# The residual gate's product in the last two blocks: seven half products in place of eight, between the first output products

## The chip, the core and the metric

The kernel runs on one core of one Trainium2 chip. The metric is the device time of one execution in microseconds (us). The engines are TensorE (PE, matmuls; its weight loads are shown apart as PEld), VectorE (DVE), ScalarE (ACT), GpSimd (POOL) and SyncE (SP, which issues transfers here).

## The reference

Attention without a softmax, an RMS norm per head, and a gated feed-forward with a gated residual:

```python
kv  = einsum('bhsd,bhse->bhde', k, v)          # 8 batches, 8 heads, 576 tokens, 64 wide
o   = einsum('bhsd,bhde->bhse', q, kv)
x   = (o / sqrt(mean(o*o, -1) + 1e-6) * g_norm) # -> 4608 tokens x 512
ffn = (gelu(x @ w_gate) * (x @ w_val)) @ w_out  # 512 -> 1536 -> 512
out = x + sigmoid(x @ w_res) * ffn              # w_res: 512 x 512
```

The change touches only `x @ w_res` and what surrounds it.

## The kernel before, in words

The 4608 tokens are worked in nine blocks of 512. Blocks 0 to 7 are the first 512 tokens of each batch; block 8 gathers the last 64 tokens of all batches. `x` lies in `xT`, transposed, in fp16: four token quarters j of 128 tokens, and four parts cc of 128 of the 512 features. Each block has two stages.

*Hidden stage.* `gv_group` (line 708) forms four of the twelve 128-wide slices of the hidden layer, for gate (g) and value (v). It uses a Strassen-Winograd scheme: a product of 2 x 2 quadrants is made with seven half products in place of eight, from sums of weight quadrants (made once) and differences of token quadrants (`token_sums`, line 688, kept in `ts`, new for each block). A half product is here four matmuls of 256 columns. The order of the work is a string of words in `ORDERS` (line 703): a digit and a factor is a half product ("6g"), E is a copy by ACT that seeds one PSUM bank with product 1 (line 747), d a copy by ACT to SBUF (line 751), F and c additions by DVE (line 758), "g11" a gelu by ACT (line 768), "h11" the product of gate and value (line 774, on DVE, and for "h22" on POOL). The last group's order ends "... 4g g12 h12 4v g21 h22 h21". Lists keyed by a word (`amid`) hang other work behind it.

*Output stage.* `m_res` (line 412) forms `x @ w_res` for one token quarter with four matmuls of 512 columns (line 415, tile `rps`) and ACT takes the tanh of half of it into `th` (line 424). Later `m_sigmoid` (line 427) turns that into a sigmoid (line 429). `out_by_products` (line 497) then forms the output product with w_out, also in seven half products, but these have twelve matmuls of 256 columns each (`prod`, line 484, matmuls on line 488): A, D, A, E, A, F, A by the names of the tiles. They read the hidden layer itself (`a_of`) or four sums of its quadrants, `hid_s`, made by DVE on line 463, each 128 x 1536: s2 in `s_begin` (line 470, hung at word "h12" of the last group), s0 and s1 in `s_rest` (line 475), s3 in `s_last` (line 481). ACT copies A to E (line 515, `wE`) and D to SBUF (line 518, `wd`); DVE adds A and `wd` to F (`wF`).

`out_last` (line 577) does the same for block 8, with smaller pieces at the end: the copies are lines 612 and 614, POOL makes `u` from `th`, `wd` and x, DVE gates (line 589), POOL or DVE add x (line 593), and SP and ACT each issue four stores (line 598), in the order in which the pieces are done.

Nothing is planned by a scheduler: each engine runs its instructions in the order of the program text, and waits on the others through semaphores. PSUM has eight banks; `banks_of` (line 1263) names those of blocks 7 and 8 by hand. In these two blocks, `LAST` on line 644, no attention work is left, and the four `rps` tiles have banks of their own. The order on PE around the change is: last group's 4g, 4v; sixteen `rps` matmuls; products A, D, A, E, A, F, A. On ACT: gelu of "g21", four tanh, copy `wE`, copy `wd`, four sigmoids (in block 8: four tanh, two sigmoids, two half copies of `w`, `wd`, two sigmoids). On DVE: h11, h12, s2, h21, s0, s1, s3.

Of the kernel before, what the change touches and what calls it, by code (L numbers as in the profile page):

```python
# [8 lines left out]
FP32 = mybir.dt.float32  # L9
FP16 = mybir.dt.float16  # L10
# [8 lines left out]
def kernel(  # L19
# [15 lines left out]
    nc = tc.nc  # L35
# [439 lines left out]
    def s_rest(blk):  # L475
# [2 lines left out]
        sub(nc.vector, s_[0], a_of(blk, 2, 1), a_of(blk, 2, 2), ALU.add)  # L478
        sub(nc.vector, s_[1], s_[0], a_of(blk, 1, 1))

    def s_last(blk):
        sub(nc.vector, hid_sums[3], a_of(blk, 1, 2), hid_sums[1])

    def prod(ps, a, b, start, es=(0, 1)):

        for e in es:
            for f in range(NFH):
# [6 lines left out]
                    skip_group_check=True,  # L494
                )

    def out_by_products(blk, later, banks, amid):
        w = {}
        s_ = hid_sums

        def aside(ahead_of):
            for f in amid.get(ahead_of, ()):
                f()

        def res(jj):
            for j in (2 * jj, 2 * jj + 1):
                m_res(blk, j, banks[j])

        def first_two():
            for n in ("D", "E", "F", "A"):  # L510
                w[n] = pmoe.tile([P, 2, CH], FP32, name="w" + n, bank=banks[n])
            w["d"] = attnp.tile([P, 2, CH], FP32, tag="sq", bufs=3, name="wd")
            s_last(blk)
# [24 lines left out]
        def others():  # L538


            prod(w["A"], s_[1], wo_t[:, 1], False)
            aside("F")
            sub(nc.vector, w["F"], w["A"], w["d"], ALU.add)
            aside("00")
            prod(w["E"], a_of(blk, 1, 2), b_of(2, 1), False)
            pf((0, 0), w["E"])
            aside("22")
            prod(w["A"], s_[2], wo_t[:, 2], False)
            c22 = res_all[part((1, 1))]
# [12 lines left out]
            if later:  # L562
                return
            for i in (1, 0):
                fin((i, i))
                fin((i, 1 - i))
                store(i)

        if later:
            x = [lambda j=j: a_x(blk, j) for j in range(NJ)]  # L570
            at_word(blk + 1, 0, "1v", *x[0:2], lambda: fin((0, 0)), lambda: fin((0, 1)), lambda: store(0))
            at_word(blk + 1, 0, "Fv", x[2])
            at_word(blk + 1, 0, "cv", x[3])
            at_word(blk + 1, 0, "h22", lambda: fin((1, 0)), lambda: fin((1, 1)), lambda: store(1))
        return [lambda: res(0), lambda: res(1), first_two, others]

    def out_last(blk, banks):

        s_ = hid_sums

        def bank(n, i):
            return pmoe.tile([P, n, CH], FP32, name="w", bank=i)

        def part(j, n, ch):
            return slice(None), slice(j, j + n), slice(ch * CH, (ch + 1) * CH)

        def gated(j, n, ch, src):
            of = part(j, n, ch)
            nc.vector.tensor_tensor(out=res_all[of], in0=th_all[of], in1=src, op=ALU.mult)

        def plus(j, n, ch, eng):
            of = part(j, n, ch)
            eng.tensor_tensor(out=res_all[of], in0=res_all[of], in1=t_t[blk][of], op=ALU.add)

        def store(j, n, c0, c1):
            for e, queue in enumerate((nc.sync, nc.scalar)):
                dst = out.rearrange("(j e s) c -> e s j c", e=2, s=S)[e, M0:S, j : j + n, c0:c1]
                queue.dma_start(out=dst, in_=res_all[e * R : (e + 1) * R, j : j + n, c0:c1])

        def run():  # L600
            wa = [bank(1, banks["A"][e]) for e in range(2)]
            wd, we, wf = [bank(2, banks[n]) for n in "DEF"]
            d = attnp.tile([P, 2, CH], FP32, tag="sq", bufs=3, name="wd")
            u = attnp.tile([P, 2, CH], FP32, tag="sq", bufs=3, name="u")
            one = (slice(0, 1), slice(1, 2))
            s_last(blk)
            for e in range(2):
                prod(wa[e], a_of(blk, 1, 1), b_of(1, 1), True, (e,))
            for j in (2, 3):
                m_sigmoid(j)  # L610
            for e in range(2):
                nc.scalar.copy(out=we[:, one[e], :], in_=wa[e])
            prod(wd, s_[0], wo_t[:, 0], True)
            nc.scalar.copy(out=d, in_=wd)
# [12 lines left out]
            gated(0, 2, 1, wf)  # L627
            plus(0, 2, 1, nc.gpsimd)
            store(0, 2, CH, C)
            for e in range(2):  # L630
                prod(wa[e], s_[2], wo_t[:, 2], False, (e,))
                gated(2 + e, 1, 1, wa[e])
            of = part(2, 2, 1)
            sub(nc.vector, res_all[of], res_all[of], u, ALU.add)
            store(2, 2, CH, C)
            for e in range(2):
                prod(wa[e], a_of(blk, 2, 2), wo_t[:, 3], False, (e,))
                gated(2 + e, 1, 0, wa[e])
                plus(2 + e, 1, 0, nc.vector)
            store(2, 2, 0, CH)  # L640

        return [lambda: [m_res(blk, j, banks[j]) for j in range(NJ)], run]

    LAST = (B - 1, B)
    GF = 4
# [526 lines left out]
    def at_word(blk, i, word, *fs):  # L1172
        amid_gv.setdefault((blk, i), {}).setdefault(word, []).extend(fs)
# [80 lines left out]
    for blk in GROUPS:  # L1254
        t = token_sums(blk, nc.vector)
        if blk == 2:
            at(blk - 1, NF + 3, *t)
            continue
        for key, f in zip(("00", "00", "22", "01") if whole(blk) else ("00", "22", "01", "11"), t):
            aside_out(blk - 1, key, f)  # L1260
    out_at = {}

    def banks_of(blk):
# [35 lines left out]
    for blk in range(B + 1):  # L1299
# [21 lines left out]
        else:  # L1321
            slots = [lambda f=f: m_gval(blk, f) for f in range(NF)]
            groups = GROUPS.get(blk, ())
            if groups:
                n = NF - GF * len(groups)
                slots[n:] = [None] * (NF - n)
                ends = []
                at_word(blk, len(groups) - 1, "h12", lambda: s_begin(blk))

                def group(i, blk=blk, ends=ends):  # L1330
                    if i == 0:
# [20 lines left out]
                plan.setdefault(NFH + 2, []).insert(0, lambda: s_begin(blk))  # L1352

            def products(blk=blk, outs=outs):
                s_rest(blk)
                if blk not in GROUPS:
                    out_at[blk] = banks_behind()
                if blk < B:
                    outs.extend(out_by_products(blk, blk == 1, out_at[blk], amid_out.get(blk, {})))
                else:  # L1360
                    outs.extend(out_last(blk, out_at[blk]))
# [54 lines left out]
```

## Time and profile before

| what | us |
|---|---|
| median of three runs (324.31 to 324.40) | 324.36 |
| the profiled execution, its own time | 324.4 |
| its span | 322.6 |
| PE busy | 314.9 |
| DVE busy | 263.5 |
| ACT busy | 201.5 |
| POOL busy | 144.9 |
| `rps` stage of block 7, starts | 273.40 to 276.86 |
| `rps` stage of block 8, starts | 304.37 to 307.82 |

How to read the rows that follow: a timeline row has start, duration, engine, line, operation, output <- inputs, shape and count. Where the engine had been idle, brackets give how long and which engine's instruction ended the wait. A matmul row's duration includes a modelled drain: rows in a stream overlap, and the pace is read from start to start. Rows of stretches (windows) have, after the engines' busy times, the granted PE clock, the share of the 16 DMA engines that was busy, and GB/s.

### The profile page before, as it was taken

The page shows a single profiled execution, that of the slowest core. Times are in us where ns is not written, and L with a number is a line of the kernel's source. Part 1 is how long each engine was busy: PE and PEld are TensorE (multiplying, and loading weights), DVE is VectorE, ACT ScalarE, POOL GpSimd, SP SyncE. Part 2 cuts the span into 40 slices and gives each one's busy share as a digit, 9 for nine tenths or more (in the row PEclk, how much of TensorE's full clock was granted, in tenths as well). Part 3 has the DMA queues.
Part 4 walks back from the last instruction along what each step waited for, and adds up shares of the span by engine and source line. Part 5 has one row for each costly group of instructions (what it writes and reads, how often), then busy time and mean ns, then how long its engine had stood idle before and what let it go on. Part 6 is the DMA issues. An engine that isn't in the chain of part 4 may idle for free.

```text
span 322.6 us, 7458 instructions
## 1 busy us (share of the span) xinstructions
PE 314.9 (98%) x2936; PEld 236.6 (73%) x2936; DVE 263.5 (82%) x482; ACT 201.5 (62%) x367; POOL 144.9 (45%) x212
## 2 busy tenths in 40 slices
PE   8999999999999999999999999999999999999993
PEld 3555754444857878887888688868887888788782
DVE  5788869799799887998799879998896777677754
ACT  3773676365737784878486848684766467636760
POOL 2792342573702779247833784117511342042232
PEclk9999999999999999999999999999999999999998
DMA  8999999798995599399938993810321030002004
GB/s 255 325 204 204 194 205 180 168 193 121 162 130 108 170 139 101 122 165 123 108 132 162 112 121 131 136 33 2 130 47 36 2 130 4 0 34 101 0 2 130
DMA packets 76693, 38.89 MB, mean 121 GB/s; under 512 B 42098, under 2 KB 74354, under 8 KB 76658
## 3 DMA queue, kind: packets, MB, share of 16 engines
q0 software_dynamic: 38752, 17.17, 42.5%
q1 hardware_dynamic: 37328, 20.71, 24.9%
q8 instruction: 23, 0.38, 0.5%
q10 hardware_dynamic: 578, 0.52, 0.5%
q14 instruction: 12, 0.10, 0.1%
HBM read 38.80 MB, written 9.44 MB: 150 GB/s over the span
## 4 chain that ended last, share of the span: by engine, by line
PE 96%; DVE 3%; issue 0%; DVEq 0%
PE Av L737 12%; PE Ag L737 12%; PE wA L488 11%; PE rps L415 10%; PE gps L395 6%; PE vps L395 6%; PE Fv L737 6%; PE Fg L737 6%; PE fps L432 3%; PE Ev L737 3%; PE wE L488 3%; PE wD L488 3%; PE Eg L737 3%; PE wF L488 3%; PE w L488 2%; PE idle L902 2%
## 5 line engine op out<-in xcount | busy, mean ns | idle before, releaser
L774 POOL TENSOR_TENSOR hid<-ge,c 128x512 f16<-128x512 f16 x21 | 24.4, 1163 | 68.5 <-ACT ge L768 68.5
L531 POOL TENSOR_TENSOR osb<-osb,t 128x512 f32<-128x512 f32 x28 | 31.6, 1159 | 36.1 <-DVE osb L527 25.2
L488 PEld LDWEIGHTS <-hid_s 128*128 128x128 f16 x384 | 37.5, 98 | 4.4
L737 PEld LDWEIGHTS <-wsv 128*128 128x128 f16 x336 | 32.8, 98 | 4.4
L737 PEld LDWEIGHTS <-wsg 128*128 128x128 f16 x336 | 32.8, 98 | 3.8
L415 PE MATMUL rps<-wr,xT 128*128 128x512 f16 x144 | 33.4, 380 | 0.0
L488 PEld LDWEIGHTS <-hid 128*128 128x128 f16 x288 | 28.2, 98 | 5.0
L747 ACT COPY Eg<-Ag 128x512 f32<-128x512 f32 x21 | 12.2, 582 | 25.9 <-PE Ag L737 25.9
L758 DVE TENSOR_TENSOR Fg<-Ag,d 128x512 f32<-128x512 f32 x21 | 14.6, 697 | 16.5 <-ACT d L751 11.2
L383 ACT ACTIVATE ge<-gps 128x512 f16<-128x512 f32 x24 | 14.1, 597 | 21.3 <-PE gps L395 21.1
L737 PEld LDWEIGHTS <-wg 128*128 128x128 f16 x252 | 24.4, 98 | 3.7 <-issue 0.4
L737 PEld LDWEIGHTS <-wv 128*128 128x128 f16 x252 | 24.6, 98 | 3.3 <-issue 0.2
L424 ACT ACTIVATE th<-rps 128x512 f32<-128x512 f32 x36 | 21.1, 595 | 8.1 <-PE rps L415 8.0
L737 PE MATMUL Ag<-ts,wsg 128*128 128x256 f16 x168 | 25.2, 273 | 0.0
L737 PE MATMUL Av<-ts,wsv 128*128 128x256 f16 x168 | 25.2, 272 | 0.0
L254 DVE TENSOR_REDUCE ss<-sq 128x8 f32<-128x512 f32 x32 | 20.1, 678 | 5.8 <-ACT sq L249 5.8
L415 PEld LDWEIGHTS <-xT 128*128 128x128 f16 x144 | 13.5, 98 | 14.2
L395 PE MATMUL gps<-xT,wg 128*128 128x512 f16 x88 | 22.6, 379 | 0.0
L395 PE MATMUL vps<-xT,wv 128*128 128x512 f16 x88 | 22.6, 379 | 0.0
L488 PE MATMUL wA<-wo_ts,hid_s 128*128 128x256 f16 x168 | 20.6, 273 | 0.0
L384 DVE TENSOR_TENSOR hid<-ge,vps 128x512 f16<-128x512 f16 x24 | 16.3, 684 | 4.8 <-PE vps L395 4.0
L429 ACT ACTIVATE th<-th 128x512 f32<-128x512 f32 x36 | 20.1, 642 | 0.0
(188 smaller groups left out, 764.7 us busy)
## 6 DMA issues: line engine op xcount, KB each, us to landing
out_dram<-osb SPq DMA_DIRECT2D x14, 512.0 KB, 2.6
qraw<-in_q_dram POOLq DMA_DIRECT2D x7, 512.0 KB, 7.1
k<-in_k_dram POOLq DMA_DIRECT2D x7, 512.0 KB, 10.2
v<-in_v_dram POOLq DMA_DIRECT2D x7, 512.0 KB, 11.4
wg<-in_moe_w_gate_dram POOLq DMA_DIRECT2D x2, 512.0 KB, 8.3
wv<-in_moe_w_val_dram POOLq DMA_DIRECT2D x2, 512.0 KB, 8.8
wo<-in_moe_w_out_dram POOLq DMA_DIRECT2D x2, 512.0 KB, 14.2
out_dram<-osb SPq DMA_DIRECT2D x4, 256.0 KB, 4.9
```

Of the source, the lines that this page charges most:

```text
L254: nc.vector.tensor_reduce(out=out_, in_=sqs.pop((b, i)), op=ALU.add, axis=mybir.AxisListType.X)
L383: nc.scalar.activation(out=ge, in_=gps, func=AF.Gelu)
L384: nc.vector.tensor_tensor(out=hids[blk][:, f, :], in0=ge, in1=vps, op=ALU.mult)
L395: nc.tensor.matmul(ps[:, j0 * P : j1 * P], lhsT=w[:, cc, :], rhs=xT_t[blk][:, j0:j1, cc, :], start=(cc == 0 and j0 == 0), stop=(cc == NP - ...
L415: nc.tensor.matmul(rps, lhsT=xT_t[blk][:, j, cc, :], rhs=wr16[:, cc, :], start=(cc == 0), stop=(cc == NP - 1),)
L424: nc.scalar.activation(out=th, in_=rps, func=AF.Tanh, scale=0.5)
L429: nc.scalar.activation(out=th, in_=th, func=AF.Copy, scale=0.5, bias=0.5)
L488: nc.tensor.matmul(ps[:, e - es[0], :], lhsT=a[:, f, e * P : (e + 1) * P], rhs=b[:, f, :], start=(start and e == es[0] and f == 0), stop=( ...
L531: nc.gpsimd.tensor_tensor(out=res_all[of], in0=res_all[of], in1=t_t[blk][of], op=ALU.add)
L737: nc.tensor.matmul(out_[:, r, :], lhsT=lhsT, rhs=rhs, start=(first and r == 0 and c == 0), stop=(c == 1), skip_group_check=True,)
L758: nc.vector.tensor_tensor(out=dst, in0=ps["A", u], in1=sb["d", u], op=ALU.add)
L774: eng.tensor_tensor(out=dst, in0=ge[q], in1=source(q, "v"), op=ALU.mult)
```

## The change

In blocks 7 and 8, `x @ w_res` is made with the seven-product scheme too (`res_halves`), and its products are laid among the first w_out products.

- Four sums of w_res quadrants (`wr_sums`) are made once, by DVE in block 6, ahead of that block's w_out product D; they lie in the buffer of `qT`, which the attention no longer uses.
- The token differences `ts` of the block are used again.
- The order is the string in `res_halves`; a number is a half product of four matmuls of 256 columns. "sE" and "sd" are ACT copies, "+F" and "+c" DVE additions, "tE" and so on the tanh of a quadrant. Behind "6" comes s0, behind "+F" s1 and the first w_out product A with its copy `wE`, behind "+c" s2 and s3, behind "tF" the first half of the w_out product D. After the string come the second half of D, the copy `wd` and the sigmoids. In block 8, where the two sigmoids of quarters 2 and 3 stood ahead of the copies of `w`, these copies now come first, then the four tanh, the two sigmoids, and then `wd`.
- `s_begin`, `s_rest` and `s_last` are no longer called for these blocks; `s_sum(blk, i)` makes s0 to s3 one at a time. The order on DVE becomes h11, h12, h21, s0, rF, s1, rc, s2, s3.
- On PE: products 1, 5, 6; w_out product A; 2, 7, 3; half of D; 4; the other half of D. From there on as before.
- POOL's and SP's instructions and their order stay the same.

```diff
+    def wr_sums(eng):
+        def one(n, x, y, op=ALU.subtract):
+            if n == 0:
+                wr_s.append(attnp.tile([P, 4, 2, CH], FP16, tag="qT", bufs=1, name="wrs"))
+            x_, y_ = (wr_s[0][:, t] if isinstance(t, int) else wr_quadrant(*t) for t in (x, y))
+            sub(eng, wr_s[0][:, n], x_, y_, op)
...
+    def res_halves(blk, banks, amid):
...
+        def product(p):
+            n = {1: "A", 2: "E", 3: "F", 4: "A", 5: "F", 6: "A", 7: "A"}[p]
...
+            for e in range(2):
+                for cc in range(2):
+                    nc.tensor.matmul(
+                        out_[:, e, :],
+                        lhsT=x_[:, e, cc, :],
+                        rhs=w_[:, cc, :],
...
+        for word in "1 sE 5 sd 6 +F 2 tE 7 +c 3 tF 4 tc tA".split():
+            n = word[-1]
+            if word.isdigit():
+                product(int(word))
+            elif word == "sE":
+                nc.scalar.copy(out=bank("E"), in_=ps["A"])
+            elif word == "sd":
+                sb["d"] = attnp.tile([P, 2, CH], FP32, tag="sq", bufs=3, name="rd")
+                nc.scalar.copy(out=sb["d"], in_=ps["F"])
+            elif word[0] == "+":
...
+                nc.vector.tensor_tensor(out=bank("F") if n == "F" else sb["c"], in0=ps["A"], in1=sb["d"], op=ALU.add)
+            else:
+                tanh(n)
+            for f in amid.get(word, ()):
+                f()
...
+        def with_res():
+            res_halves(blk, dict(zip("AFE", (banks[j] for j in range(3)))), {
+                "6": [lambda: s_sum(blk, 0), tiles_of_w],
+                "+F": [lambda: s_sum(blk, 1), lambda: prod(w["A"], a_of(blk, 1, 1), b_of(1, 1), True),
+                       lambda: nc.scalar.copy(out=w["E"], in_=w["A"])],
+                "+c": [lambda: s_sum(blk, 2), lambda: s_sum(blk, 3)],
+                "tF": [lambda: half_d(0)],
+            })
+            half_d(1)
+            nc.scalar.copy(out=w["d"], in_=w["D"])
+            for j in range(NJ):
+                m_sigmoid(j)
...
+        if res_in_halves(blk):
+            return [with_res, lambda: None, lambda: None, others]
         return [lambda: res(0), lambda: res(1), first_two, others]
...
+            res_halves(blk, dict(zip("AFE", (banks[j] for j in range(3)))), {
+                "6": [lambda: s_sum(blk, 0)],
+                "+F": [lambda: s_sum(blk, 1), ahead],
+                "+c": [lambda: s_sum(blk, 2), lambda: s_sum(blk, 3)],
+                "tF": [lambda: half_d(0)],
+            })
...
-            s_last(blk)
-            for e in range(2):
-                prod(wa[e], a_of(blk, 1, 1), b_of(1, 1), True, (e,))
+            half_d(1)
             for j in (2, 3):
                 m_sigmoid(j)
-            for e in range(2):
-                nc.scalar.copy(out=we[:, one[e], :], in_=wa[e])
-            prod(wd, s_[0], wo_t[:, 0], True)
             nc.scalar.copy(out=d, in_=wd)
...
-        return [lambda: [m_res(blk, j, banks[j]) for j in range(NJ)], run]
+        return [lambda: None, run]
...
+    aside_out(LAST[0] - 1, "D", *wr_sums(nc.vector))
...
-                at_word(blk, len(groups) - 1, "h12", lambda: s_begin(blk))
+                if not res_in_halves(blk):
+                    at_word(blk, len(groups) - 1, "h12", lambda: s_begin(blk))
...
-                s_rest(blk)
+                if not res_in_halves(blk):
+                    s_rest(blk)
```

More of the change, by code (lines that the diff above doesn't have):

```diff
@@ L479, in s_rest, with s_sum @@
         sub(nc.vector, s_[1], s_[0], a_of(blk, 1, 1))
+    def s_sum(blk, i):
+        s_ = hid_sums
+        if i == 0:
+            sub(nc.vector, s_[0], a_of(blk, 2, 1), a_of(blk, 2, 2), ALU.add)
+        elif i == 1:
+            sub(nc.vector, s_[1], s_[0], a_of(blk, 1, 1))
+        elif i == 2:
+            sub(nc.vector, s_[2], a_of(blk, 1, 1), a_of(blk, 2, 1))
+        else:
+            sub(nc.vector, s_[3], a_of(blk, 1, 2), s_[1])
     def s_last(blk):
@@ L495, in prod, with wr_quadrant @@
                 )
+    wr_s = []
+    def wr_quadrant(i, k):
+        return wr16[:, 2 * k : 2 * k + 2, i * CH : (i + 1) * CH]
+    def wr_sums(eng):
[4 more added lines that the diff above has]
+            sub(eng, wr_s[0][:, n], x_, y_, op)
+        return [
+            lambda: one(0, (1, 0), (1, 1), ALU.add),
+            lambda: one(1, 0, (0, 0)),
+            lambda: one(2, (0, 0), (1, 0)),
+            lambda: one(3, (0, 1), 1),
+        ]
@@ new lines, in res_halves, with bank, tanh @@
+    def res_halves(blk, banks, amid):
+        ps, sb = {}, {}
+        def bank(n):
+            ps[n] = pmoe.tile([P, 2, CH], FP32, name="r" + n, bank=banks[n])
+            return ps[n]
+        def product(p):
+            n = {1: "A", 2: "E", 3: "F", 4: "A", 5: "F", 6: "A", 7: "A"}[p]
+            first = p in (1, 5)
+            out_ = bank(n) if first else ps[n]
+            s_of = {3: 3, 5: 0, 6: 1, 7: 2}
+            t_of = {4: 3, 5: 0, 6: 1, 7: 2}
+            quad = {1: (0, 0), 2: (0, 1), 4: (1, 1)}
+            xq = {1: (0, 0), 2: (1, 0), 3: (1, 1)}
+            w_ = wr_s[0][:, s_of[p]] if p in s_of else wr_quadrant(*quad[p])
+            x_ = x_sums[blk][:, t_of[p]] if p in t_of else x_quadrant(blk, *xq[p])
+            for e in range(2):
[4 more added lines that the diff above has]
+                        rhs=w_[:, cc, :],
+                        start=(first and e == 0 and cc == 0),
+                        stop=(cc == 1),
+                        skip_group_check=True,
+                    )
+        def tanh(n):
+            i, j = {"E": (0, 0), "F": (0, 1), "A": (1, 0), "c": (1, 1)}[n]
+            src = sb[n] if n == "c" else ps[n]
+            th = th_all[:, 2 * j : 2 * j + 2, i * CH : (i + 1) * CH]
+            nc.scalar.activation(out=th, in_=src, func=AF.Tanh, scale=0.5)
+        for word in "1 sE 5 sd 6 +F 2 tE 7 +c 3 tF 4 tc tA".split():
[8 more added lines that the diff above has]
+            elif word[0] == "+":
+                if n == "c":
+                    sb["c"] = attnp.tile([P, 2, CH], FP32, tag="o32", bufs=3, name="rc")
+                nc.vector.tensor_tensor(out=bank("F") if n == "F" else sb["c"], in0=ps["A"], in1=sb["d"], op=ALU.add)
+            else:
+                tanh(n)
+            for f in amid.get(word, ()):
+                f()
@@ L497, in out_by_products, with res_in_halves @@
+    def res_in_halves(blk):
+        return blk in LAST
     def out_by_products(blk, later, banks, amid):
@@ L507, in res, with tiles_of_w @@
                 m_res(blk, j, banks[j])
-        def first_two():
+        def tiles_of_w():
             for n in ("D", "E", "F", "A"):
@@ L512, in first_two, with half_d @@
             w["d"] = attnp.tile([P, 2, CH], FP32, tag="sq", bufs=3, name="wd")
+        def half_d(e):
+            prod(w["D"][:, e : e + 1], s_[0], wo_t[:, 0], e == 0, (e,))
+        def with_res():
[10 more added lines that the diff above has]
+                m_sigmoid(j)
+        def first_two():
+            tiles_of_w()
             s_last(blk)
@@ L600, in run, with ahead, half_d @@
         def run():
-            wa = [bank(1, banks["A"][e]) for e in range(2)]
-            wd, we, wf = [bank(2, banks[n]) for n in "DEF"]
+            wa, w = [], []
+            one = (slice(0, 1), slice(1, 2))
+            def ahead():
+                wa.extend(bank(1, banks["A"][e]) for e in range(2))
+                w.extend(bank(2, banks[n]) for n in "DE")
+                for e in range(2):
+                    prod(wa[e], a_of(blk, 1, 1), b_of(1, 1), True, (e,))
+                for e in range(2):
+                    nc.scalar.copy(out=w[1][:, one[e], :], in_=wa[e])
+            def half_d(e):
+                prod(w[0][:, one[e], :], s_[0], wo_t[:, 0], e == 0, (e,))
+            res_halves(blk, dict(zip("AFE", (banks[j] for j in range(3)))), {
[4 more added lines that the diff above has]
+            })
+            wd, we = w
+            wf = bank(2, banks["F"])
             d = attnp.tile([P, 2, CH], FP32, tag="sq", bufs=3, name="wd")
             u = attnp.tile([P, 2, CH], FP32, tag="sq", bufs=3, name="u")
-            one = (slice(0, 1), slice(1, 2))
-            s_last(blk)
-            for e in range(2):
-                prod(wa[e], a_of(blk, 1, 1), b_of(1, 1), True, (e,))
+            half_d(1)
             for j in (2, 3):
                 m_sigmoid(j)
-            for e in range(2):
-                nc.scalar.copy(out=we[:, one[e], :], in_=wa[e])
-            prod(wd, s_[0], wo_t[:, 0], True)
             nc.scalar.copy(out=d, in_=wd)
```

## The prediction

> **What bounds the kernel now.** I read the page's busy shares and slices, then its chain, then TensorE's (PE's) timeline over the last three blocks, then the other engines around the two stages that change.
>
> ```profile
> PE 314.9 (98%) x2936; PEld 236.6 (73%) x2936; DVE 263.5 (82%) x482; ACT 201.5 (62%) x367; POOL 144.9 (45%) x212
> PEclk9999999999999999999999999999999999999998
> PE 96%; DVE 3%; issue 0%; DVEq 0%
> ```
>
> PE is busy for 98% of the span, at full granted clock, and holds 96% of the chain that ended last. An instruction taken from PE shortens the run only if PE does not wait somewhere else instead. The stage in block 7:
>
> ```profile
> 272.53 0.60 PE L737 MATMUL Ag<-ts,wg 128*128 128x256 f16 x4
> 272.97 0.60 PE L737 MATMUL Av<-ts,wv 128*128 128x256 f16 x4
> 273.40 3.62 PE L415 MATMUL rps<-wr,xT 128*128 128x512 f16 x16
> 276.86 1.47 PE L488 MATMUL wA<-wo,hid 128*128 128x256 f16 x12
> 278.17 1.47 PE L488 MATMUL wD<-wo_ts,hid_s 128*128 128x256 f16 x12
> 279.48 1.47 PE L488 MATMUL wA<-wo_ts,hid_s 128*128 128x256 f16 x12
> ```
>
> The starts give the pace: 16 matmuls of 512 columns in 276.86-273.40 = 3.46 us (216 ns each); 12 of 256 columns in 1.31 us (109.2 ns each). Block 8 has the same rows from 304.37. No row has an idle note: PE does not wait in this stage. Below, t is the time from the first w_res matmul of a block.
>
> ```profile
> 273.23 0.59 ACT L768 ACTIVATE ge<-Ag 128x512 f16<-128x512 f32 x1
> 286.66 0.57 ACT L747 COPY Eg<-Ag 128x512 f32<-128x512 f32 x1 [4.32 <-PE Ag L737]
> 287.15 0.58 ACT L747 COPY Ev<-Av 128x512 f32<-128x512 f32 x1
> ```
>
> The second row prices a seed copy: its four matmuls start at 286.03, so ScalarE (ACT) starts 0.63 after them and takes 0.57. Queued ACT copies start 0.49 apart. PE's one wait for another engine's eviction in the steady part shows what follows:
>
> ```profile
> 102.66 0.68 DVE L758 TENSOR_TENSOR c<-Ag,d 128x512 f32<-128x512 f32 x1
> 103.27 0.67 DVE L758 TENSOR_TENSOR c<-Av,d 128x512 f32<-128x512 f32 x1
> 103.39 0.60 PE L737 MATMUL Ag<-ts,wg 128*128 128x256 f16 x4 [0.18 <-DVE c L758]
> 103.99 0.60 PE L737 MATMUL Av<-ts,wv 128*128 128x256 f16 x4
> ```
>
> VectorE (DVE) ends at 103.34, PE starts at 103.39: 0.05 from an eviction's end to the matmul that waited.
>
> **The change, part by part.**
>
> *Matmuls.* Per block 16 of 512 columns go (3.46) and 28 of 256 columns come (28 x 0.1092 = 3.06). That is 0.40 less on PE, 0.80 over two blocks, all on the path. [...]
>
> *The new wait.* The words "1 sE 5 sd 6": product 1 fills bank A, ACT copies A to E, product 6 then adds onto A, so it must wait until that copy has read A; the compiled order has this wait on ACT. In the gate and value groups the other factor's products stand between; here only product 5 does. Product 1 runs t = 0 to 0.437, product 5 to 0.873. The copy starts at 0.63 (the last gelu before it, 273.23 + 0.59, is off ACT by t = 0.42) and ends at 1.20; PE goes on at 1.25. PE thus loses 1.25 - 0.873 = 0.38 per block, 0.76 in all. Bounds: 0.31 (a copy of 0.55, the shortest in that stretch, and PE on at its end) and 0.64 (0.10 more if a weight load has not gone ahead, 0.16 more if the 0.60 from 103.39 to 103.99 is a restart). I take 0.38: the 0.60 has a nearer reason, the second addition, which ends at 103.94. Behind product 6 stand all later matmuls.
>
> *The rest of the stage.* Product 6 ends at 1.69, the w_out product A at 3.00. Product 7 comes at 3.44 and needs the addition rF on DVE: h21 at 0.57, the sum s0 at 1.16 (0.95), rF at about 2.1 to 2.85. It is in time by 0.5. Product 3 follows, half of D from 4.31 to 4.97, then product 4, which needs rc: product 7's start 3.44 + 0.63 = 4.07, 0.69 long, 0.05: 4.81. In time by 0.16. The other half of D ends at 6.06, against 3.46 + 2.62 = 6.08 before. The sums s2 and s3, now last on DVE, end near 6.7; their products come at 8.7 or later. The DVE additions (two of 0.7 per block) and ACT copies (two of 0.6) lie in this slack; what exceeds it, PE waits for one to one ahead of product 4. In block 6 the four differences of w_res (0.41 each as the token differences' rows, 1.65 in all) stand on DVE ahead of wF, which had 2.77 of idle before it: nothing, and only what exceeded 2.77 would reach PE, at the F product. They read a weight long loaded, into the buffer of qT, free since block 5. POOL and SP get no instruction and none moves in their order.
>
> *The last block's tail.* Before, ACT did the sigmoids of token quarters 2 and 3 ahead of the D product, and copied wd at once:
>
> ```profile
> 308.51 1.14 ACT L429 ACTIVATE th<-th 128x512 f32<-128x512 f32 x2
> 310.64 0.59 ACT L614 COPY wd<-w 128x512 f32<-128x512 f32 x1 [0.33 <-PE w L488]
> ```
> ```profile
> 311.30 1.27 POOL L463 TENSOR_TENSOR u<-th,wd 128x512 f32<-128x512 f32 x1 [6.25 <-ACT wd L614]
> 312.65 1.15 POOL L463 TENSOR_TENSOR u<-u,t 128x512 f32<-128x512 f32 x1
> 314.08 2.41 POOL L593 TENSOR_TENSOR osb<-osb,t 128x512 f32<-128x512 f32 x2 [0.28 <-DVE osb L589]
> ```
>
> Now the tanh of A waits for product 4 (4.97 + 0.63 = 5.60), the two sigmoids follow at 6.1 and 6.6, wd at 7.15, ending at 7.74; before it ended at t = 6.86. Three followers:
> - DVE's two halves of wF end near 8.57, PE needs them at 8.69 and its weight load a little sooner: 0.05, bounds 0 and 0.35.
> - The sigmoids of quarters 0 and 1 end at 8.79, the gating of E starts at 8.9 as before: nothing.
> - POOL's u moves 0.88 later. POOL had 0.28 idle ahead of its additions, so these and the first two stores move by 0.6. The last store is issued by DVE's end (318.68) and stays, but the transfers run into each other:
>
> ```profile
> 317.75:318.00 0.25, 0.00 (x0) 0.00 (x0) 0.25 (x2) 0.00 (x0) 0.00 (x0) 1.00 0.37 111
> 319.25:319.50 0.25, 0.00 (x0) 0.00 (x0) 0.00 (x0) 0.00 (x0) 0.00 (x0) 1.00 0.99 287
> 319.75:320.00 0.25, 0.00 (x0) 0.00 (x0) 0.00 (x0) 0.00 (x0) 0.00 (x0) 0.53 0.17 49
> ```
>
> The column before the last is the DMA share: from 316.6 to 321.1 the engines are nearly full, with only about 0.16 + 0.21 us of gaps. A start 0.6 later minus those gaps ends 0.25 later. Bounds: 0 (the last store overtakes) and 0.64.
>
> *Sum.* Against the profiled execution (324.4: 322.6 of span, 1.8 around it; the median of three is 324.36): 324.40 - 0.80 + 0.76 + 0.05 + 0.25 = 324.66. With all bounds low: 324.40 - 0.80 + 0.62 = 324.22; all high: 324.40 - 0.80 + 1.28 + 0.35 + 0.64 = 325.87.
>
> **Rivals.**
> 1. *The saving is kept.* If product 6 did not wait, 324.40 - 0.80 = 323.60, or 323.85 with the tail's delay. Against it: 0.44 us cannot cover a drain and a copy of 1.25 us in any row here. For it: only that the modelled ends of matmuls may be off.
> 2. *Slower: a restart after each wait.* Place: product 6 in both blocks. If a wait also costs the 0.16 and the 0.10 of the bound above, it is 0.64 and not 0.38: 324.66 + 0.52 = 325.18. It decides from a wait of 0.56 on, where the total passes 325.01. For it the 0.60 after 103.39, against it that row's nearer reason.
> 3. *ACT becomes the bound in the last block.* If thA, two sigmoids and wd run at full duration (0.60, 0.64, 0.64, 0.59) and not 0.5 apart, wd ends at 8.08, wF near 9.0, and PE waits 0.35 for it in place of 0.05: 324.66 + 0.30 = 324.96. Against it: the rows show starts 0.48 to 0.53 apart wherever ACT has a queue.
>
> **Numbers.** A measurement of this kernel can tell 0.2% (0.65 us) from no change: 323.71 to 325.01. Chances: my forecast 0.70, near 324.66, with its own range 324.2 to 325.0; rival 1 0.08 (faster); rival 2 0.12 (slower); rival 3 0.10, of which 0.04 ends above 325.01. So faster 0.08, same 0.76, slower 0.16. The range 324.0 to 325.2 takes in the forecast, rival 3 and about half of rival 2, and leaves out rival 1.
>
> **What would show it.** In the changed profile: 28 matmuls per block at 109 ns; an idle note on the first matmul of product 6 that names ACT's rE copy, its start 1.25 after product 1's; no idle note on products 7, 3 and 4; the second half of D ending at t = 6.06; wd in the last block at t = 7.15; u on POOL 0.9 later; the first store at about 315.9 and DMA without its two gaps. I am wrong if PE waits on DVE ahead of product 4 (the thinnest margin, 0.16), if product 6 starts much before or after 1.25, or if the last transfer lands when it did.

## The result, and the profile after

| | median us (range, runs) | profiled execution, us | its span | opening | rest |
|---|---|---|---|---|---|
| before | 324.36 (324.31 to 324.40, 4) | 324.40 | 322.6 | 37.28 | 285.32 |
| changed | 325.63 (325.54 to 326.43, 4) | 325.68 | 323.9 | 37.95 | 285.95 |

The changed kernel is slower: the ratio is 1.0045, with a 95% interval of 1.0027 to 1.0062. The forecast was 324.66 and its range ended at 325.2. (Of all executions here two, of 835.7 us in `again` and 410.6 in `only7`, were far longer than the others; the ratios leave them out, the medians count them.)

The table cuts the span in two. The *opening* ends where block 0's sixteen w_res matmuls start on PE (tile `rps`, the same in both kernels); it holds the first loads, the attention of batch 0 and the first hidden stage. The *rest* goes from there to the end of the span. The change touches nothing in the opening, yet 0.67 of the 1.3 us lies there; the rest grew by 0.63. The two are taken up apart. (Spans are read to 0.1, so a rest is good to 0.05; with each execution's own time in place of its span, the differences to before come out the same within 0.05.)

First the rest. The page of the changed kernel, its busy line and the shares of the chain that ended last:

```profile
PE 314.6 (97%) x2960; PEld 239.3 (74%) x2960; DVE 267.9 (83%) x490; ACT 203.3 (63%) x371; POOL 144.9 (45%) x212
PE 95%; DVE 3%; ACT 0%; issue 0%; DVEq 0%; ACTq 0%
```

PE has 24 more matmuls (32 go, 56 come) and is busy for 0.3 us less, in a span that is 1.3 longer: it stood still for longer. From PE's list of waits (engine, tile and line, the releaser; total us, times, longest):

```profile
PE rA L548 <- ACT rE L568: 0.6, 2, 0.3
```

That is the wait which the forecast named, once in each of the last two blocks. In block 7, from PE's timeline:

```profile
274.08 0.60 PE L548 MATMUL rA<-wr,xT 128*128 128x256 f16 x4
274.52 0.60 PE L548 MATMUL rF<-wrs,ts 128*128 128x256 f16 x4
275.39 0.60 PE L548 MATMUL rA<-wrs,ts 128*128 128x256 f16 x4 [0.28 <-ACT rE L568]
275.82 1.47 PE L500 MATMUL wA<-wo,hid 128*128 128x256 f16 x12
277.13 0.60 PE L548 MATMUL rE<-wr,xT 128*128 128x256 f16 x4
277.57 0.60 PE L548 MATMUL rA<-wrs,ts 128*128 128x256 f16 x4
278.01 0.60 PE L548 MATMUL rF<-wrs,xT 128*128 128x256 f16 x4
278.44 0.82 PE L500 MATMUL wD<-wo_ts,hid_s 128*128 128x256 f16 x6
279.10 0.60 PE L548 MATMUL rA<-wr,ts 128*128 128x256 f16 x4
279.54 0.82 PE L500 MATMUL wD<-wo_ts,hid_s 128*128 128x256 f16 x6
280.19 1.47 PE L500 MATMUL wA<-wo_ts,hid_s 128*128 128x256 f16 x12
```

The rows are products 1, 5, 6, the w_out product A, 2, 7, 3, half of D, 4, the other half of D, and the next A. Start to start, four matmuls take 0.44, as before (109 ns each). Only the row of product 6 has an idle note. Its matmuls start 0.87 after product 5's in place of 0.437, so the loss is 0.43; the bracket says 0.28, because the modelled drain of product 5 still counts as busy. Product 6 starts at t = 1.31, and the second half of D ends at t = 280.19 - 274.08 = 6.11, where the old stage ended at 6.08. Why product 6 starts then is in ACT's timeline:

```profile
273.91 0.59 ACT L890 ACTIVATE ge<-Ag 128x512 f16<-128x512 f32 x1
274.77 0.57 ACT L568 COPY rE<-rA 128x512 f32<-128x512 f32 x1 [0.28 <-PE rA L548]
```

The gelu ahead is done at 274.50; the seed copy waits for product 1's end, starts at t = 0.69, and ends at 275.34, 0.05 before product 6. Block 8 shows the same distances from 305.08. Its tail, from the timeline of all engines:

```profile
312.27 0.58 ACT L736 COPY wd<-w 128x512 f32<-128x512 f32 x1
312.50 1.47 PE L500 MATMUL w<-wo,hid 128*128 128x256 f16 x12
...
312.88 0.97 DVE L463 TENSOR_TENSOR w<-w,wd 128x256 f32<-128x256 f32 x2 [1.25 <-ACT wd L736]
312.93 1.27 POOL L463 TENSOR_TENSOR u<-th,wd 128x512 f32<-128x512 f32 x1 [7.16 <-ACT wd L736]
313.91 1.48 PE L500 MATMUL w<-wo,hid_s 128*128 128x256 f16 x12
...
315.39 2.27 POOL L701 TENSOR_TENSOR osb<-osb,t 128x512 f32<-128x512 f32 x2
...
317.27 0.94 DVE L463 TENSOR_TENSOR osb<-osb,u 128x512 f32<-128x512 f32 x1
...
319.36 0.43 DVE L701 TENSOR_TENSOR osb<-osb,t 128x256 f32<-128x256 f32 x1
```

In the kernel before, the same two DVE additions were:

```profile
316.41 0.69 DVE L463 TENSOR_TENSOR osb<-osb,u 128x512 f32<-128x512 f32 x1
...
318.25 0.43 DVE L593 TENSOR_TENSOR osb<-osb,t 128x256 f32<-128x256 f32 x1
```

Read from the top: `wd` starts 7.19 after the block's product 1 and ends at 7.77. DVE's two halves of wF end at 313.85, and PE, due with the F product at 312.50 + 1.31 = 313.81, starts it at 313.91. POOL's u is 0.92 later against the block's start (t = 7.85, before 6.93). The DVE addition of u to `osb`, which took 0.69 before, takes 0.94: POOL's last two additions, which used to end 0.08 after it began (316.49), now run until 317.66, 0.39 into it. DVE's last addition ends at 319.79, before at 318.68: 1.11 later. Of that 0.67 is the opening, 0.06 the two stages, 0.13 the F product's wait (0.10, the rest is rounding and 0.01 behind it), 0.25 the long addition. The end of the span is 1.30 later, so the stores add 0.19.

### The profile page after: what moved, and what is told of

It reads as the page before. It is cut to its first block, busy times and chain, and to the rows that moved or that the text cites. A ratio compares the mean times of both kernels' runs of the same rounds, so it can differ in the third digit from the quotient of the medians.

```text
span 323.9 us, 7525 instructions
## 1 busy us (share of the span) xinstructions
PE 314.6 (97%) x2960; PEld 239.3 (74%) x2960; DVE 267.9 (83%) x490; ACT 203.3 (63%) x371; POOL 144.9 (45%) x212
## 4 chain that ended last, share of the span: by engine, by line
PE 95%; DVE 3%; ACT 0%; issue 0%; DVEq 0%; ACTq 0%
PE Av L859 12%; PE Ag L859 12%; PE wA L500 11%; PE rps L415 8%; PE gps L395 6%; PE vps L395 6%; PE Fv L859 6%; PE Fg L859 6%; PE fps L432 3%; PE wF L500 3%; PE wE L500 3%; PE wD L500 3%; PE Ev L859 3%; PE Eg L859 3%; PE w L500 2%; PE idle L1024 2%
## 5 line engine op out<-in xcount | busy, mean ns | idle before, releaser
L415 PE MATMUL rps<-wr,xT 128*128 128x512 f16 x112 | 26.2, 380 | 0.0
L424 ACT ACTIVATE th<-rps 128x512 f32<-128x512 f32 x28 | 16.3, 594 | 5.2 <-PE rps L415 5.1
L890 ACT ACTIVATE ge<-Eg 128x512 f16<-128x512 f32 x21 | 12.5, 597 | 9.5 <-PE Eg L859 9.5
## 6 DMA issues: line engine op xcount, KB each, us to landing
k<-in_k_dram POOLq DMA_DIRECT2D x7, 512.0 KB, 10.1
```

The lines of the kernel that those rows point to most:

```text
L415: nc.tensor.matmul(rps, lhsT=xT_t[blk][:, j, cc, :], rhs=wr16[:, cc, :], start=(cc == 0), stop=(cc == NP - 1),)
L424: nc.scalar.activation(out=th, in_=rps, func=AF.Tanh, scale=0.5)
```

## The experiments

Opening and rest are read from each kernel's own profile. Two theories on the opening were told apart beside the terms of the rest. **Theory P**: the late opening belongs to the changed program. **Theory C**: it is a matter of the single execution, and the same instructions can have either.

| kernel | opening | rest | median us (runs) | ratio to before, 95% interval |
|---|---|---|---|---|
| again (changed, unaltered) | - | - | 325.20 (11) | 1.0020, 1.0011 to 1.0029 |
| sums | 37.44 | 285.36 | 324.46 (12) | 1.0003, 0.9993 to 1.0013 |
| only7 | 37.10 | 285.40 | 324.36 (11) | 0.9997, 0.9988 to 1.0007 |
| only8 | 37.12 | 285.88 | 324.91 (11) | 1.0015, 1.0004 to 1.0027 |
| hide | 37.16 | 285.04 | 324.11 (11) | 0.9993, 0.9983 to 1.0003 |
| tail | 37.38 | 285.52 | 324.71 (11) | 1.0008, 0.9999 to 1.0017 |
| hidetail | 37.42 | 284.68 | 323.76 (11) | 0.9980, 0.9971 to 0.9988 |
| again2 (changed, unaltered) | 37.79 | 286.01 | 325.51 (6) | 1.0026, 1.0015 to 1.0038 |
| base (before, unaltered) | 37.11 | 285.39 | 324.27 (1) | - |
| again3 (changed, unaltered) | 37.92 | 286.98 | 325.14 (12) | 1.0015, 1.0003 to 1.0028 |
| warm4 | 37.46 | 285.94 | 324.98 (12) | 1.0002, 0.9992 to 1.0012 |
| hidetail4 | 37.12 | 284.68 | 323.61 (12) | 0.9972, 0.9957 to 0.9986 |

The kernel before, run beside them, had medians of 324.42 (first four), 324.45 (next four) and 324.57 (last four). `again` has no opening and rest, since its profiled execution was the one of 835.7 us.

### Which part costs what: sums, only7, only8, again

`sums` is the kernel before with only the four sums of w_res added; `only7` and `only8` make the change in one of the two blocks; `again` is the changed kernel.

```diff
 def res_in_halves(blk):
-    return blk in LAST
+    return False
```

That is `sums`; `only7` returns `blk == LAST[0]`, `only8` returns `blk == B`. For `sums` and `only7` the function that runs block 8's end is that of before.

> The kernel before plus only the four sums of w_res on VectorE in block 6. Both theories: they are hidden, rest 285.3. P says that the opening goes with the program, which is almost that before: 37.3, time 324.3 to 324.4. C: opening anywhere from 37.2 to 38.2, time 324.3 to 325.3.

> The seven half products in block 7 alone, block 8 as before. My reading of the two profiles: the wait of product 6 eats the saving in block 7 (+0.03 us measured), so rest 285.35, with product 6 starting 1.31 us after product 1. The rival that half products do save by themselves in a block that is not the last: rest 284.95 (-0.4). Opening: not foreseen; P puts it between 37.28 and 37.95, C anywhere.

> The seven half products in block 8 alone. My reading: +0.03 in its stage, then 0.12 of waiting for wF, 0.25 from a VectorE addition that runs beside POOL's late additions, and 0.2 from stores that are issued later: rest 285.9. The rival that these losses need both blocks: rest 285.4. Opening as for the other kernels: P between 37.28 and 37.95, C anywhere.

> The changed kernel once more, nothing edited. Two stretches are kept apart: the opening (start of the sixteen w_res matmuls of block 0, whose instructions the change does not touch: 37.28 us before, 37.95 after) and the rest (from there to the end of the span: 285.32 before, 285.95 after). Theory P, the later opening belongs to this program: opening near 37.95 again, time 325.5 to 325.7. Theory C, the opening is drawn anew by chance with each load: it may come back at 37.3, and the time then is 324.9 to 325.0. Both: rest 285.9 to 286.0.

The rests are 285.36, 285.40 and 285.88; those of the kernel before are 285.32 and, in `base`, 285.39. So the four DVE sums cost nothing, and the stage of block 7 costs about nothing: its 0.40 of saved matmuls is eaten by its wait of 0.43. Block 8 costs about 0.5, nearly the whole change, and since its stage is that of block 7, this is the tail. The parts add up: 285.35 + 0.05 + 0.53 = 285.93, and 285.95 was measured.

The times of `again` spoke against theory P in its strict form: with the same program, five of the eleven times lie at 324.81 to 324.97 and five between 325.2 and 325.61 (the last is the one of 835.7).

### Taking the wait away: hide

Half of the w_out product A is laid between products 5 and 6, in both blocks, so that PE has work while ACT copies.

```diff
-    "6": [lambda: s_sum(blk, 0), tiles_of_w],
-    "+F": [lambda: s_sum(blk, 1), lambda: prod(w["A"], a_of(blk, 1, 1), b_of(1, 1), True),
-           lambda: nc.scalar.copy(out=w["E"], in_=w["A"])],
+    "sd": [tiles_of_w, lambda: prod(w["A"][:, 0:1], a_of(blk, 1, 1), b_of(1, 1), True, (0,))],
+    "6": [lambda: prod(w["A"][:, 1:2], a_of(blk, 1, 1), b_of(1, 1), False, (1,)), lambda: s_sum(blk, 0)],
+    "+F": [lambda: s_sum(blk, 1), lambda: nc.scalar.copy(out=w["E"], in_=w["A"])],
...
```

These are the lines for block 7; those for block 8 do the same with its smaller pieces.

> The first half of the w_out product A (six matmuls, 0.66 us) stands between products 5 and 6, the second half behind product 6; nothing else is edited against the changed kernel. My theory, PE loses 0.43 us per block because only product 5 stands between the seed copy and product 6: product 6 starts 1.53 us after product 1 with no idle note, the second half of D ends at t = 5.7 and not 6.11, and the rest (from the start of block 0's sixteen w_res matmuls to the end of the span; 285.95 in the changed kernel, 285.32 before) is 285.1. Rival, the wait moves on to product 7 or 4 because VectorE's sums are then late: t = 6.0 to 6.1 again, rest 285.8 to 285.9. Time, if the opening is as in most runs of the kernel before (37.1 to 37.4): 324.1 by the first, 324.8 by the second.

PE's rows of `hide` in block 7, from product 5 to product 2:

```profile
273.72 0.60 PE L548 MATMUL rF<-wrs,ts 128*128 128x256 f16 x4
274.16 0.82 PE L500 MATMUL wA<-wo,hid 128*128 128x256 f16 x6
274.81 0.60 PE L548 MATMUL rA<-wrs,ts 128*128 128x256 f16 x4
275.25 0.82 PE L500 MATMUL wA<-wo,hid 128*128 128x256 f16 x6
275.91 0.60 PE L548 MATMUL rE<-wr,xT 128*128 128x256 f16 x4
```

Product 6 (third row) has no idle note, and nothing behind it has one: the wait is gone and did not move on to product 7 or 4. The second half of D ends at 5.67 in place of 6.11, 0.44 sooner. Two blocks would give 0.88, and the rest fell by 0.91 (285.95 to 285.04). That settles the first main step: the seven-product scheme does save 0.40 per block, and the wait on ACT's seed copy took it all.

### The tail of the last block: tail, and both together: hidetail

In `tail`, block 8 runs the second half of D straight behind product 4, and ACT does the sigmoids of quarters 2 and 3 and then `wd` ahead of the tanh of A, which moves behind them. (wF gets the bank that is free, since F's own waits for the tanh.) `hidetail` has both edits.

```diff
+    def behind():
+        half_d(1)
+        for j in (2, 3):
+            m_sigmoid(j)
...
+        nc.scalar.copy(out=w_d[0], in_=w[0])
...
+        "tc": [behind],
...
-    wf = bank(2, banks["F"])
+    wf = bank(2, banks[3])
...
-    half_d(1)
-    for j in (2, 3):
-        m_sigmoid(j)
-    nc.scalar.copy(out=d, in_=wd)
```

> Only the last block's tail is edited: on ScalarE the two sigmoids of quarters 2 and 3 and the copy wd stand ahead of the tanh of A, the second half of D directly behind product 4 as before, and wF lies in a bank of its own. My theory, the late wd costs 0.56 us in the end (0.12 of PE waiting for wF, 0.25 for a VectorE addition beside POOL's late additions, 0.19 in the stores): u starts on POOL at t = 7.3 and not 7.85, the last VectorE addition with u takes 0.69 and not 0.94, rest 285.4. Rival, the loss comes from the smaller pieces of the stage themselves, not from wd: rest 285.9.

> Both edits together. If both theories hold and do not overlap: rest 284.6, that is 0.7 under the kernel before, time 323.6 to 323.8 with an opening of 37.1 to 37.4, faster than both kernels. If the wait only moves to product 7 or 4, rest 285.3; if the tail's loss is not from wd, rest 285.1.

The tail of `tail`, same columns as that of the changed kernel above:

```profile
311.29 0.56 ACT L730 COPY wd<-w 128x512 f32<-128x512 f32 x1
...
311.89 0.97 DVE L463 TENSOR_TENSOR w<-w,wd 128x256 f32<-128x256 f32 x2 [0.81 <-ACT wd L730]
...
311.94 1.47 PE L500 MATMUL w<-wo,hid 128*128 128x256 f16 x12
...
313.25 1.47 PE L500 MATMUL w<-wo,hid_s 128*128 128x256 f16 x12
...
314.40 2.28 POOL L701 TENSOR_TENSOR osb<-osb,t 128x512 f32<-128x512 f32 x2
...
316.60 0.69 DVE L463 TENSOR_TENSOR osb<-osb,u 128x512 f32<-128x512 f32 x1
```

`wd` now starts 6.77 after product 1 (304.52). The F product starts 1.31 behind its predecessor, on time. POOL's additions end at 316.68, and DVE's addition, begun at 316.60, is back at 0.69. The rest fell by 0.43 (285.52): 0.25 by that addition, 0.10 by the F product, 0.08 by the stores. Of the tail's 0.57 (0.13, 0.25 and 0.19 above) 0.14 is still there, most of it in the stores.

The 0.94 is not chance: the addition takes 0.94 or 0.95 in the profiles of all kernels with block 8's new order and without this edit (changed, only8, hide, again2, again3, warm4), and 0.69 in all others (before, base, sums, only7, tail, hidetail, hidetail4). In the changed kernel's profile POOL's additions reach 0.39 into it, in those of before, tail and hidetail 0.08. The size of the delay doesn't follow from the rows: POOL was busy for 0.39 of DVE's addition, and it took 0.25 longer. So the delay beside POOL is shown by the runs, its reason is not.

The gains of the two edits add up in `hidetail`: 285.95 - 0.91 - 0.43 = 284.61, and 284.68 was measured. Its ratio of 0.998 (0.9971 to 0.9988) makes it faster than both kernels.

### The opening: again2, base, again3, warm4

> The changed kernel a third time, for the opening. Theory P (the late opening belongs to this program): opening near 37.95, time 325.5. Theory C (chance of the run or the chip): opening anywhere from 37.1 to 38.0, independent of the program, rest 285.9 to 286.0, lowest time 324.8 as in the second measurement.

> The kernel before, profiled once more, unchanged. Question: does its opening (start to block 0's w_res matmuls) vary by itself, with the moment at which PE's first matmuls go to full pace? On both theories the rest (from there to the span's end) is 285.3 us. Theory C (the opening is a matter of the execution): the opening is anywhere from 37.1 to 37.95, and goes with two rows: six warm-up matmuls of 1.8 to 2.4 us give 37.1 to 37.2; of 2.77 with the first four k-v matmuls of 0.44 give 37.3; with these of 0.60 or more give 37.45 to 37.95. Theory P (the late opening belongs to the changed program): 37.1 to 37.3 again.

> The changed kernel, unchanged, for the third time. Rest 285.95. Theory C: about one time in four lies in the late group (near 325.5), as one in four of the kernel before's own lies 0.6 above its main group, and most lie at 324.8 to 325.0; the ratio is near 1.0015. Theory P: more than half lie near 325.5, median 325.3 to 325.6, ratio 1.0026 or more.

What differs in the openings is best seen in PE's first rows. Of `only7`, with an opening of 37.10:

```profile
6.49 1.81 PE L1010 MATMUL idle<-zeros 128*128 128x512 f16 x6
8.51 0.38 PE L1068 MATMUL kvp<-v,k 128*128 128x128 f16 x4 [0.20 <-DVE v L1031]
8.73 0.28 PE L1074 MATMUL kvp<-hid_s,kf 128*128 128x128 f16 x2
```

Of the kernel before, 37.28:

```profile
6.49 2.77 PE L902 MATMUL idle<-zeros 128*128 128x512 f16 x6
9.05 0.44 PE L960 MATMUL kvp<-v,k 128*128 128x128 f16 x4
9.33 0.28 PE L966 MATMUL kvp<-hid_s,kf 128*128 128x128 f16 x2
```

Of the changed kernel, 37.95:

```profile
6.49 2.77 PE L1024 MATMUL idle<-zeros 128*128 128x512 f16 x6
9.05 0.63 PE L1082 MATMUL kvp<-v,k 128*128 128x128 f16 x4
9.48 0.42 PE L1088 MATMUL kvp<-hid_s,kf 128*128 128x128 f16 x2
9.69 0.59 PE L1082 MATMUL kvp<-v,k 128*128 128x128 f16 x4
```

The `idle` rows are six warm-up matmuls on zeros, queued ahead of the first k-v product. The instructions are the same in all three kernels; the pace is not. In the changed kernel's execution four k-v matmuls take 0.43 from start to start (107 ns each), in that of `only7` 0.22 (55 ns): PE began at half pace and went to full pace at some moment after. In the changed kernel that was at 10.1 (the fourth row is still slow, the next is not), in the kernel before at 9.2 (one of the first four k-v matmuls is slow, three are not), and in `only7` near 7.1 (an estimate): six matmuls of 512 columns take 2.77 at half pace, and 1.81 leaves room for about one and a half of them at 0.43 (the warm-ups' distance from start to start in the other two), the others at 0.22 (that of the `rps` matmuls). At half pace the six hold the first k-v product until 9.05, though DVE has cast its v by 8.5 to 8.65. The granted clock in the rows of stretches is 1.00 throughout in all three, so it does not show this. What sets the moment, which lies some 3 us apart here (from 7.1 to 10.1), no run shows.

The pace makes up only half of the changed kernel's 0.67. PE's next rows are 0.30 late (the first `op` product at 10.28, before at 9.98), and at 14.38, before at 14.04, they are 0.34 late. The other 0.33 enters at the next k-v product. Before:

```profile
13.90 0.41 DVE L923 CAST v<-hid_s 128x512 f16<-128x512 f32 x1
14.37 0.38 PE L960 MATMUL kvp<-v,k 128*128 128x128 f16 x4
```

Changed:

```profile
14.24 0.74 DVE L1045 CAST v<-hid_s 128x512 f16<-128x512 f32 x1
14.70 1.31 POOL L1177 CAST wg<-wgf 128x512 f16<-128x512 f32 x2
15.04 0.38 PE L1082 MATMUL kvp<-v,k 128*128 128x128 f16 x4 [0.26 <-DVE v L1045]
```

DVE's cast of v begins 0.34 later and takes 0.33 longer, and PE waits for it; from there to the end of the opening the distance stays 0.67. In eleven of the twelve other profiles this cast takes 0.41 or 0.42, and POOL's cast of wg begins 0.29 or more after it is over; in the twelfth, `again2`, the two run into each other and it takes 0.53. So the long casts are the ones beside POOL, but the cause is open: at its usual length the cast of 0.74 would have ended at 14.65, 0.05 before POOL's begins.

Theory C holds: the same instructions have either opening. The opening of one and the same program varies: 37.28 and 37.11 for the kernel before, and `base` falls between the two pictures (warm-up 2.41). It also varies through the first loads: in `again3` the v load lets ACT and DVE cast at 8.83, not at 8.0 to 8.2, and the opening is 37.92 although its first k-v matmuls already run at full pace (0.39). `again3`'s profiled execution took 326.72, the second longest of its kind; its rest holds one more wait, of 0.62, for the w_out weights' load, and is not used for the rest. `again2` alone looked like theory P, with 37.79 and four of six times late. That the program shifts the odds of a late opening is neither shown nor excluded.

So the time has an upper group for both kernels. Of 96 times of the kernel before, 27 lie 0.6 or more above its fastest (324.2); of 32 of the changed kernel (without the one of 835.7), 14 lie 0.6 or more above its fastest (324.81), namely all of the first four, and 10 of the 28 since. `again3` alone had 3 of 12 and theory C's ratio of 1.0015; before, beside it, had 12 of 29.

`warm4` intervenes: the changed kernel with four warm-up matmuls in place of six ahead of the first k-v product.

```diff
- qc1P qc0A qT1 qT0 kc1P kc0A qo0D warm3 lk0D lv0P qo1A warm3 vc1D ...
+ qc1P qc0A qT1 qT0 kc1P kc0A qo0D warm3 lk0D lv0P qo1A warm1 vc1D ...
```

> The changed kernel with four warm-up matmuls in place of six ahead of the first k-v product. My reading: in executions with a late switch to full pace, the six matmuls at half pace (0.43 each) are what holds the k-v product until 9.05; with four it starts when its v is cast, at 8.5 to 8.7, 0.35 to 0.5 sooner, and the opening is 0.3 to 0.5 shorter (37.95 becomes 37.5); in executions with an early switch nothing changes (37.1). So the late group goes from 325.5 to 325.1, the early one stays at 324.85; median 324.8 to 325.1. Rival: the pace goes up only after PE has been busy for some time, and the idle stretch of up to 0.4 ahead of the k-v product puts that off; then the products run at half pace for longer, the opening is 38 or more and the median 325.6 or more. Rest 285.95 on both.

> The version with both repairs (half of the w_out product A between products 5 and 6; product D, two sigmoids and wd ahead of the tanh of A in the last block), with four warm-up matmuls in place of six. Rest 284.7 as without that. My reading: opening 37.1 to 37.5, median 323.5 to 323.8, and its upper group no more than 0.3 above the lower. Rival as before: opening 38 or more, median 324.3 or more.

The twelve times of `warm4` lie between 324.85 and 325.17: the lower edge of the changed kernel, without its upper group (up to 325.6 and more). Its median is 324.98, and its rest of 285.94 is that of the changed kernel. So none of its 12 times lies in the upper group, where 14 of 32 lay with six warm-up matmuls (3 of 12 in `again3`, run beside it). The rival, a still later change of pace, fell. That the queue of warm-up matmuls at half pace made that group fits these times, but it is not shown: its profiled execution is no test of it, and `hidetail4`, with four as well, has two late times. (The ratio of 1.0002 leans on before's upper group beside it; the medians give 1.0013.) In its profiled execution the product waits for its data:

```profile
6.49 1.46 PE L1024 MATMUL idle<-zeros 128*128 128x512 f16 x4
8.86 0.38 PE L1082 MATMUL kvp<-v,k 128*128 128x128 f16 x4 [0.91 <-DVE v L1045]
```

The 1.46 leaves room for two matmuls at half pace, so PE went to full pace near 7.3 (an estimate), early as in `only7`; six would have been done before the data too. The opening of 37.46 there comes with a late load of v, which ACT and DVE cast at 8.38 (`base`: 8.03 on ACT).

`hidetail4` is the fastest of all, 323.61, ratio 0.9972 (0.9957 to 0.9986); ten of its twelve times lie between 323.53 and 323.74. Two, 324.94 and 325.62, do not, so my expectation of a narrow upper group missed there; neither was profiled, and their cause is open. `hidetail`, with six warm-up matmuls, had one such time in eleven (324.81), so the 0.15 between these two medians isn't shown to come from this edit.

## Why the prediction was wrong

The terms of its sum, against what was measured (us):

| term | predicted | measured | from |
|---|---|---|---|
| matmuls saved, two blocks | -0.80 | -0.80 | 109 ns per matmul, start to start |
| wait of product 6, two blocks | +0.76 | +0.86 | 2 x (0.87 - 0.437), `hide` gives back 0.91 |
| PE's wait for wF in block 8 | +0.05 | +0.13 | F product 0.10 late, 0.01 behind it, the rest rounding |
| DVE's addition beside POOL | none | +0.25 | 0.94 for 0.69; `tail` undoes it |
| stores run into each other | +0.25 | +0.19 | span's end against DVE's end |
| sum of the rest | +0.26 | +0.63 | 285.95 - 285.32 |
| the opening | taken as unchanged | +0.67 | 37.95 - 37.28: 0.34 with the pace, 0.33 with DVE's cast |

**The step that failed** is the base of the sum, "Against the profiled execution (324.4: 322.6 of span, 1.8 around it; the median of three is 324.36): 324.40 - 0.80 + ...". It takes the opening of that one execution for the changed kernel's as well. The opening is not a property of the program alone: it ran from 37.10 to 37.95 in these profiles. The profile of before could not show this by its granted clock, but it did show the half pace: six warm-up matmuls in 2.77. Neither the range nor the rivals had a term for it. By itself it takes the forecast out of the range: 324.66 + 0.67 = 325.33. Had the opening stood, the changed kernel would have come to 324.40 + 0.63 = 325.03, inside the range of 324.0 to 325.2 and just across the bound between "same" and "slower". The repeats, with 325.20, 325.51 and 325.14, lie between, as their share of late openings has it. Why all of the first four executions fell late is open; the program's part in that was not shown. (The sum with all bounds high, 325.87, would have covered 325.63, but through terms of 1.28, 0.35 and 0.64 that measured 0.86, 0.13 and 0.19.)

**The steps that held.** The 28 matmuls run at the pace of the rows of the kernel before, 109 ns each, four in 0.44. The wait stands where it was put, names ACT's copy, and eats the saving; it was 0.05 longer per block because the copy starts 0.69 behind product 1, not 0.63; why it does is open. Products 7, 3 and 4 have no idle note, so the thin margin of 0.16 ahead of product 4 held. Rival 1 (no wait) and rival 2 (a wait of 0.56 or more) fell: 0.43 is inside the bounds of 0.31 to 0.64. The four sums in block 6 cost nothing (`sums`).

**The terms that were off in size.** The tail was put at 0.30 (0.05 and 0.25) and took 0.57. The prediction let DVE's end stay ("the last store is issued by DVE's end (318.68) and stays") and looked for the price of POOL's delay only in the transfers. But POOL's last two additions, 0.60 later as forecast (t = 10.31, before 9.71), reached into the DVE addition, and 0.25 of DVE's delay came from there. Rival 3's premise fell too: `wd` started close to the forecast (7.19 for 7.15) and ended at 7.77, not 8.08. That PE still waited 0.10 for wF comes from DVE, whose two halves end 1.00 after `wd`, where 0.83 was reckoned. The stores' gaps did not vanish: two stretches of the DMA engines of the changed kernel (last columns: granted PE clock, DMA share, GB/s) still stand half empty,

```profile
319.00:319.25 0.25, 0.00 (x0) 0.00 (x0) 0.25 (x1) 0.00 (x0) 0.00 (x0) 1.00 0.45 144
321.00:321.25 0.25, 0.00 (x0) 0.00 (x0) 0.00 (x0) 0.00 (x0) 0.00 (x0) 0.50 0.52 160
```

so the 0.19 is near the 0.25 by other means than were reckoned. The first store is issued at 316.57, which is 315.90 without the opening's 0.67, as forecast.

## What to carry to other kernels

Before counting on a scheme with fewer matmuls, look for other PE work to put in front of each product that reuses a bank still being copied: here, with 0.65 us of another product laid there, the same seven products went from a loss of 0.03 to a gain of 0.41 us per block. When a forecast is about tenths of a microsecond, first look at which part of the base run is a draw: a start at half pace (107 ns for a matmul that takes 55 at full pace), a late load (v cast at 8.83, not at 8.0 to 8.2) and a DVE cast of nearly twice its usual length (0.74 for 0.41) moved the opening by up to 0.85 us with no instruction of it changed. And when an engine off the path is delayed, ask beside which other engine's work it will run at its new time, not only whose data it delivers: here a DVE addition beside POOL's late ones took 0.94 in place of 0.69.

## What the runs showed of the hardware

- PE's change from half to full pace came anywhere from about 7 us to about 10 us in executions whose instructions up to there were the same; the granted clock read 1.00 all the while where it was read (before, changed, only7, warm4). The early ends, 7.1 and 7.3, are estimates from the length of the warm-up rows; 9.2 and 10.1 are in the rows. At half pace a matmul of 128 columns took 107 ns, at full pace 55.
- A DVE addition of 128x512 in fp32, from SBUF to SBUF, took 0.69 in seven profiles and 0.94 or 0.95 in six. POOL's additions ended 0.08 into it in the profiles of before, tail and hidetail (0.69 each), and 0.39 into it in that of the changed kernel (0.94).
- An ACT copy of PSUM released PE 0.05 after its end, and began 0.69 after the start of the four matmuls it waited for, in both blocks of the changed kernel (0.63 in the forecast's row of another copy).
